# A sliding-window attention with a gated feed-forward on one core: the branch to a general path turned round and hinted, the test's product later, the first tile's row sums elsewhere

## The chip, the cores and the metric

The kernel runs on one core of one Trainium2 chip. The core has a matrix engine (TensorE; PE in the profile, and PEld for its weight loads), three engines for elementwise work (VectorE, DVE; ScalarE, ACT; GpSimd, POOL) and an engine that mainly issues DMAs (SyncE, SP). Each runs its own list of instructions in order and waits for the others by semaphores. The metric is the device time of one execution in microseconds, as the median of several runs.

## The reference

Attention over 8 batches of 8 heads, 576 positions, 64 dimensions, where a position sees itself and the 63 before it; then a gated feed-forward over the 4608 tokens.

```
scores = scale * q @ k^T                 # scale = 1/8
scores = where(0 <= row - column < 64, scores, -1e9)
attn = exp(scores - max);  attn = attn / (sum + 1e-9)
x = (attn @ v), heads side by side       # 4608 x 512
g = x @ w_gate                           # 512 x 1536
out = (g * sigmoid(g) * (x @ w_val)) @ w_out
```

## The kernel before

**Tiles.** The tokens are worked off as nine tiles (NT = 9) of 512. Tile 0 has code of its own; tiles 1 to 6 and 8 hold 512 positions of one batch each; tile 7 (LAST) collects the last 64 positions of all batches. Of each tile the kernel makes the scores, their exponents without taking off the maximum, the row sums by a product with ones, their inverse as exp(-ln(sum)) on ACT, and the attention's output scaled by it (`xT`). Then come twelve gate steps (`gate_value`, matmuls at L470): each makes 128 of the 1536 columns of the gate and value products with eight matmuls of 512 columns, ACT makes the sigmoid-weighted gate (`sg`, L463) and DVE the product with the value (`hT`, L464). The projection with `w_out` (L479, L491, L532) of a tile lies among the next tile's attention; that of the last tile stands at the end, in four blocks of 128 tokens (`project` for three, `project_last` for the fourth), each with a copy out of the accumulator on DVE and output DMAs on SP's queue.

**Order.** The order of the instructions on each engine is that of the program text (a manual schedule). The accumulators are eight banks; a gate step takes two of the four banks 4 to 7 in turn, so the second step after it takes the same two again.

**The start.** For tile 0 the four head pairs u go one after the other: cast, transpose (L207), copy out (L714, L210), scores (L260), exponent (`weigh_first`, L719), row totals (`sums_first`, L326), logarithm (L347), inverse (`invert`, L350), the product with v (L376, L391), and the scaling (L427). The first gate matmuls (`gate_part`, L446) follow as the four parts of `xT` get done.

**The test.** Since no maximum is taken off, an exponent could run over. ACT can sum a row beside its main result (`accum_out`), which costs it a second instruction, ACTIVATION_READ_ACCUMULATOR. Every exponent and every inverse writes such a sum into a column of `spread` (`extent()` gives the next column). In gate step 4 of the last tile `survey` (L539) compares all columns with a bound, takes the minimum over them (`within`), adds the 128 partitions with one matmul of one column (L545) and casts the result into `count`. At the end of the program every engine loads the count into a register (`values_load`, L943). Where it is under 128 (`tc.If`, L944) the general path runs, a long plain version of the whole computation. For the data here it is 128, and the general path is passed over.

**The branch as it is laid out.** `preferred_fallthrough_block=False` puts the block for "not less" next: on each engine a compare-and-branch that is not taken, a few semaphore settlements (EVENT_SEMAPHORE, L944; SP's wait for its outputs to land among them), then a jump over the general path to the closing code (L972: waits, drains, the last barrier).

Of the kernel before, what the change touches and what calls it, by code (L numbers as in the profile page):

```python
# [8 lines left out]
P = 128  # L9
FP32 = mybir.dt.float32  # L10
BF16 = mybir.dt.bfloat16
AF = mybir.ActivationFunctionType
ALU = mybir.AluOpType
PSUM = bass.MemoryType.PSUM


@with_exitstack
def kernel(
# [10 lines left out]
    nc = tc.nc  # L29
    S, D, H = 576, 64, 8  # L30
    NTOK, DFF, DM = 4608, 1536, 512
    NT = NTOK // 512
# [39 lines left out]
    def extent():  # L72
        columns_used[0] += 1
        return spread[:, columns_used[0] - 1:columns_used[0]]
# [153 lines left out]
    def turn_k(dst, k_s, u):  # L228
        nc.vector.transpose(  # L229
            dst[:, u, :].rearrange("r (g x e) -> r g e x", g=4, e=4),  # L230
            k_s[:, :, u].rearrange("r g (e d) -> r g e d", d=D)[:, :, :, 0:32],
        )
# [106 lines left out]
    def room(n):  # L339
        return fsb.tile([P, 2, 512], FP32, name="r", tag="r", bufs=4)[:, 0:n]  # L340
# [5 lines left out]
    def log(r, d_ps):  # L346
        nc.scalar.activation(r, d_ps, AF.Ln, bias=floor[:])  # L347

    def invert(r):
        nc.scalar.activation(r, r, AF.Exp, scale=-1.0, accum_out=extent())  # L350

    def logs(t, r, d):
        if t == NT - 1:
# [4 lines left out]
    def sums(t, w, tiles):  # L358
        r = room(2)
        totals(t, w, tiles if len(tiles) > 1 else [tiles[0][:, x] for x in range(2)])  # L360
        for x in range(2):
            inverse[t, 2 * w + x] = r[:, x]
        if len(tiles) > 1:
            for x in range(2):
                logs(t, r[:, x:x + 1], tiles[x].rearrange("r (b x) -> r b x", b=1))
        else:
            logs(t, r, tiles[0])
        return lambda: invert(r)

    def part_first(us, x, ms, last=None):  # L370

# [94 lines left out]
    def gate_value(t, m):  # L466
        pair = gate_tiles()
        for ps, w in zip(pair, (wg, wv)):
            for c in range(4):
                nc.tensor.matmul(  # L470
                    ps[:], w[:, c, P * m:P * m + P], xT[t][:, c, :],
                    start=(c == 0), stop=(c == 3),
                )
        gate_end(t, m, pair)
# [48 lines left out]
    def project(t, s, o_ps):  # L523
        project_part(t, (s,), (o_ps,), range(12))
        project_end(t, s, o_ps)

    def project_last(t, s):
        r0 = S * batch(t) + P * s
        os_ = fsb.tile([P, 512], FP32, name="os_", tag="os_", bufs=4)
        for f0, f1, o_ps in ((0, 384, bank[6]), (384, 512, bank[0])):  # L530
            for c in range(12):
                nc.tensor.matmul(  # L532
                    o_ps[:, 0:f1 - f0], hT[t][:, c, P * s:P * s + P], wo[:, c, f0:f1],
                    start=(c == 0), stop=(c == 11),
                )
            nc.vector.tensor_copy(os_[:, f0:f1], o_ps[:, 0:f1 - f0])
            nc.sync.dma_start(out[r0:r0 + P, f0:f1], os_[:, f0:f1])

    def survey():  # L539

        used = spread[:, 0:columns_used[0]]
        fine = fsb.tile([P, 64], FP32, name="fine", tag="fine", bufs=1)[:, 0:columns_used[0]]
        nc.vector.tensor_single_scalar(fine, used, MOST, op=ALU.is_le)
        nc.vector.tensor_reduce(within[:, 0:1], fine, axis=mybir.AxisListType.X, op=ALU.min)
        nc.tensor.matmul(two[0][:, 0, 0:1], ones[:, 0:P], within[:, 0:1])  # L545
        nc.vector.tensor_copy(count[:], two[0][:, 0, 0:1])

# [168 lines left out]

    def weigh_first(u):
        E = eb[u][:, 1:17].rearrange("r (h y) z -> r h (y z)", h=2)
        nc.scalar.activation(E, two[u % 2][:], AF.Exp, scale=0.125, accum_out=extent())  # L719
        weights[0, u] = E  # L720

    def sums_first(u, b):
        totals_first(u, bank[b])
        inverse[0, u] = room(1)[:, 0]
        return lambda: log(inverse[0, u], bank[b]), lambda: invert(inverse[0, u])

    cast_first(on_a, 0, 0)
    cast_first(on_v, 0, 1)
# [83 lines left out]
    for m in range(12):  # L812
        if m < 4:
            if m == 2:
                pairs += [gate_tiles(), gate_tiles()]
                for i, w in enumerate((wg, wv)):
                    for n in (2, 3):
                        for c in range(4):
                            gate_one(0, n, pairs[n][i], w, c)
            gate_end(0, m, pairs[m])  # L820
        else:
            gate_value(0, m)
        if m == 3:
            for x in range(2):
                for c in range(2):
                    nc.vector.tensor_copy(
                        mask[half(x), 0, c],
                        tri[half(x), x ^ c].rearrange("r (y e) -> r e y", e=16),
                    )
            for i in (1, 2, 4):  # L830
                nc.vector.tensor_copy(mask[:, i:2 * i], mask[:, 0:i])
            for E in eb:
                nc.vector.memset(E[:, 0], 0.0)
        if m == 10:
            for u in range(4):
                tp = two[u % 2].bitcast(BF16)[:, u // 2, 0:512]
                for e in range(4):
                    for h in range(2):
                        nc.tensor.transpose(  # L839
                            tp[half(h), P * e:P * e + P], raw_k[:, 2 * u + h, e], identb[:]  # L840
                        )
            for u in range(4):
                tp = two[u % 2].bitcast(BF16)[:, u // 2, 0:512]
                split_k(kT[1][:, u, :], tp, on_a if u % 2 else on_v)
        if m == 8:
            second_halves(1, lo, 1, on_v)
            second_halves(1, lo, 0, on_a)
        if m == 9:
            for u in range(2):
                turn_q(1, u)  # L850
# [34 lines left out]
    for t in range(1, NT):  # L885
        if t > 1:
            set_exp()
            masks = scores(t, 0)
            masks[0]()
            project_quads(t - 1, tiles, range(12), 0)  # L890
            for x in range(2):
                marker(4 + 2 * x, x)
            on_a(fence[:], bank[4][0:D, 0:1])
            on_v(seen[:], bank[6][0:D, 0:1])
            masks[1]()
            if t == 2:
                stage_v(3)
            ready(scores(t, 1))
            for x in range(2):
                marker(4 + 2 * x, x)  # L900
            project_quads(t - 1, tiles, range(7), 1)
            end = sums(t, 0, two[0:1])
            project_quads(t - 1, tiles, range(7, 12), 1)
            for w in range(2):
                mix_half(t, w, two[1 - w])
            project_end(t - 1, 0, tiles[0], on_a)
            ends = end, sums(t, 1, (bank[4], bank[6]))
            for end in ends:
                end()
            project_end(t - 1, 2, tiles[2])  # L910
            project_part(t - 1, (1,), (bank[5],), range(12))
            scale_all(t, (two[1], two[0]))
            project_end(t - 1, 1, bank[5], on_a)
            project_part(t - 1, (3,), (bank[4],), range(12))
        set_silu()
        if t > 1:
            project_end(t - 1, 3, bank[4], on_v)
        on_p(past[:], xT[t][:, 3, 0:1])  # L918
        if t + 1 == LAST:
            load_last_v()  # L920
        elif t + 1 < NT and t > 1:
            cast_v(t + 1)
        if t + 2 < NT:
            load_qk(t + 2)
            if t > 1 and t + 2 != LAST:
                stage_v(t + 2)
        if t == 2:
            k_l = cast.tile([P, 4, 4, 4 * D], BF16, name="k_l", tag="c0")
        if t in (2, 3):
            load_k(k_l, [(b, S - P) for b in range(4, 8)], quarters[2 * t - 4:2 * t - 2])  # L930
        turns = (6, 7, 9, 10) if t == 1 else (1, 4, 7, 10)
        for m in range(12):
            gate_value(t, m)
            if t == NT - 1 and m == 4:
                survey()
            if m in turns and t + 1 < NT:
                turn(t + 1, turns.index(m))
            if (t, m) in late:
                turn_k(kT[2], k_l, late.index((t, m)))
    for s in range(3):  # L940
        project(NT - 1, s, bank[(5, 7, 4)[s]])
    project_last(NT - 1, 3)
    good = nc.values_load(count[0:1, 0:1], min_val=0, max_val=P)  # L943
    with tc.If(good < P, preferred_fallthrough_block=False):  # L944
        for b in range(8):
            x_b = general_attention(b)
            general_ffn(b, x_b)
# [29 lines left out]
```

## Time and profile before

| | us |
|---|---|
| median of 3 runs | 330.51 (330.12 to 330.61) |
| the profiled execution's own time | 330.77 |
| its span | 329.05 |
| PE busy | 315.8 |
| first gate matmul starts | 16.07 |
| last matmul ends | 320.85 |
| last copy ends | 321.16 |

The span runs from the first to the last instruction of the program; the execution's own time holds 1.72 us around it. "Busy" counts matmuls, elementwise work and POOL's DMA writing; branches, register loads and semaphore instructions are not counted, so a stretch in which all engines stand at 0 can still be full of these. In the trace such instructions stand under the engine's name with a q (SPq, PEldq). The granted clock of TensorE is 0.993 over the span.

### The profile page before, as it was taken

To read this page: it belongs to the slowest core of one execution; us is meant where nothing else is said; L and a number is where in the kernel's file an instruction comes from. 1 tells how busy PE (TensorE), PEld (TensorE's weight loads), DVE (VectorE), ACT (ScalarE), POOL (GpSimd) and SP (SyncE) were. 2 spreads that over 40 slices of the span, in tenths; PEclk is the share of its full clock that TensorE was granted. 3 is DMA by queue.
4 is the path that set the end of the run, shared out by engine and by line. 5 is a ranking of instruction groups with operands and counts; after the bars stand their busy time and mean duration, and the time that the engine had idled before them with its cause. 6 is when DMAs were issued, how large, how long until landed. Compare 5 with 4: busy or idle time off the path is not lost.

```text
span 329.0 us, 8172 instructions
## 1 busy us (share of the span) xinstructions
PE 315.8 (96%) x3298; PEld 158.9 (48%) x3298; DVE 209.7 (64%) x345; ACT 177.1 (54%) x295; POOL 147.7 (45%) x268
## 2 busy tenths in 40 slices
PE   7899999999999999999999999999999999998990
PEld 3544444446444644464446444644455445543450
DVE  4855846596667657674778477858875587643330
ACT  4964765358534863486338733873377336932200
POOL 3965656867667156624560399027870200000000
PEclk9999999999999999999999999999999999999997
DMA  7999999999699349944991489249995200120031
GB/s 221 213 195 198 208 140 228 200 199 125 124 205 186 52 100 190 193 56 121 170 180 19 120 108 110 29 106 171 178 145 104 54 0 2 47 85 2 1 100 40
DMA packets 83537, 40.53 MB, mean 123 GB/s; under 512 B 64161, under 2 KB 78753, under 8 KB 83489
## 3 DMA queue, kind: packets, MB, share of 16 engines
q0 software_dynamic: 51488, 22.59, 57.4%
q1 hardware_dynamic: 31456, 16.79, 22.6%
q8 instruction: 28, 0.46, 0.6%
q10 hardware_dynamic: 544, 0.52, 0.5%
q14 instruction: 21, 0.16, 0.2%
HBM read 53.02 MB, written 9.44 MB: 190 GB/s over the span
## 4 chain that ended last, share of the span: by engine, by line
PE 94%; DMA 1%; ACT 1%; DVE 1%; issue 0%; DVEq 0%
PE one L470 55%; PE one L479 17%; PE one L491 11%; PE two L289 3%; PE two L411 2%; PE one L446 2%; DMA q_f<-in_q_dram 1%; ACT eb L719 1%; PE two L333 1%; PE one L532 1%; PE two L446 1%; PE one L333 1%; ACT qk_b L705 0%; PE two L839 0%; PE one L207 0%
## 5 line engine op out<-in xcount | busy, mean ns | idle before, releaser
L463 ACT ACTIVATE sg<-one 128x512 f32<-128x512 f32 x107 | 63.9, 597 | 115.7 <-PE one L470 90.2
L464 DVE TENSOR_TENSOR hT<-sg,one 128x512 bf16<-128x512 f32 x107 | 74.0, 693 | 62.9 <-PE one L470 59.3
L470 PE MATMUL one<-xT,wg 128*128 128x512 bf16 x416 | 106.8, 379 | 0.0
L470 PE MATMUL one<-xT,wv 128*128 128x512 bf16 x416 | 106.8, 379 | 0.0
L138 POOL DMA_DIRECT2D k_s<-in_k_dram x112 | 60.5, 563 | 26.6 <-DMA q_s<-in_q_dram 14.9
L470 PEld LDWEIGHTS <-wg 128*128 128x128 bf16 x416 | 40.6, 98 | 50.1 <-issue 1.5
L470 PEld LDWEIGHTS <-wv 128*128 128x128 bf16 x416 | 40.7, 98 | 49.0
L479 PE MATMUL one<-wo,hT 128*128 128x512 bf16 x252 | 56.5, 379 | 0.0
L918 POOL COPY past<-xT 128x1 bf16<-128x1 bf16 x8 | 1.5, 189 | 88.9 <-DVE xT L427 88.9
L491 PE MATMUL one<-wo,hT 64*64 64x512 bf16 x672 | 40.4, 376 | 0.0
L479 PEld LDWEIGHTS <-hT 128*128 128x128 bf16 x252 | 23.8, 98 | 29.3 <-issue 2.0
L229 DVE STREAM_TRANSPOSE kT<-k_s 128x512 bf16<-128x512 bf16 x28 | 36.0, 1287 | 0.0
L427 DVE TENSOR_TENSOR xT<-two,r 128x512 bf16<-128x512 f32 x34 | 21.2, 683 | 22.4 <-ACT r L350 22.4
L304 ACT ACTIVATE eb<-two 128x960 bf16<-128x960 f32 (+1 forms) x32 | 31.0, 973 | 3.8 <-PE two L289 3.7
L491 PEld LDWEIGHTS <-hT 64*64 64x64 bf16 x672 | 21.7, 107 | 10.8
L310 DVE TENSOR_TENSOR eb<-eb,mask 128x960 bf16<-128x960 bf16 (+1 forms) x32 | 21.0, 655 | 8.0 <-ACT eb L304 8.0
L219 DVE STREAM_TRANSPOSE qT<-q_s 128x512 bf16<-128x512 bf16 x32 | 22.3, 700 | 0.1
L350 ACT ACTIVATE r<-r 128x1024 f32<-128x1024 f32 (+1 forms) x20 | 19.3, 970 | 0.1
L315 DVE TENSOR_TENSOR both<-eb 128x512 bf16<-128x512 bf16 x32 | 13.6, 426 | 1.1
L103 POOL DMA_DIRECT2D q_s<-in_q_dram x24 | 13.0, 555 | 2.0 <-DMA v<-in_v_dram 1.1
L164 POOL DMA_DIRECT2D vb<-in_v_dram x16 | 11.0, 693 | 6.1 <-DMA wo<-in_moe_w_out_dram 3.7
L347 ACT ACTIVATE r<-one,floor 128x512 f32<-128x512 f32 x17 | 10.9, 683 | 4.0 <-PE one L333 4.0
(146 smaller groups left out, 259.1 us busy)
## 6 DMA issues: line engine op xcount, KB each, us to landing
k_s<-in_k_dram POOLq DMA_DIRECT2D x112, 56.0 KB, 5.3
q_s<-in_q_dram POOLq DMA_DIRECT2D x24, 248.0 KB, 5.9
v_f<-in_v_dram SPq DMA_DIRECT2D x40, 128.0 KB
wg<-in_moe_w_gate_dram POOLq DMA_DIRECT2D x5, 256.0 KB, 8.1
wv<-in_moe_w_val_dram POOLq DMA_DIRECT2D x5, 256.0 KB, 8.7
q_f<-in_q_dram SPq DMA_DIRECT2D x4, 256.0 KB
wo<-in_moe_w_out_dram POOLq DMA_DIRECT2D x2, 512.0 KB, 10.8
vb<-in_v_dram POOLq DMA_DIRECT2D x16, 64.0 KB, 6.4
```

What stands on the lines that cost most here:

```text
L138: nc.gpsimd.dma_start(k_s[p0:p0 + 32, g, :, 0:w], k[b, a:H:2, s:s + P].rearrange("u (r e) d -> r u (e d)", e=4) [:, :, 32 * c:32 * c + w],)
L219: nc.vector.transpose(queries[t][:, u, :].rearrange("r (e x) -> r e x", e=16), staged[t][0][:, u].rearrange("r (e d) -> r e d", d=D)[:, :, ...
L229: nc.vector.transpose(dst[:, u, :].rearrange("r (g x e) -> r g e x", g=4, e=4), k_s[:, :, u].rearrange("r g (e d) -> r g e d", d=D)[:, :, ...
L304: nc.scalar.activation(flat, s_ps[:].rearrange("r a b -> r (a b)")[:, 0:n], AF.Exp, scale=0.125, accum_out=extent(),)
L310: nc.vector.tensor_mul(flat, flat, mask[:].rearrange("r j c e y -> r (j c e y)")[:, 0:n])
L350: nc.scalar.activation(r, r, AF.Exp, scale=-1.0, accum_out=extent())
L427: nc.vector.tensor_mul(x, o_ps, r)
L463: nc.scalar.activation(sg[:], g_ps[:], AF.Silu)
L464: nc.vector.tensor_mul(hT[t][:, m, :], sg[:], v_ps[:])
L470: nc.tensor.matmul(ps[:], w[:, c, P * m:P * m + P], xT[t][:, c, :], start=(c == 0), stop=(c == 3),)
L479: nc.tensor.matmul(o_ps[:], hT[t][:, c, P * s:P * s + P], wo[:, c, :], start=(c == 0), stop=(c == 11),)
L491: nc.tensor.matmul(tiles[s][half(y)], hT[t][half(x), c, r0:r0 + 64], wo[half(x), c, :], start=not back and c == 0, stop=bool(back) and c = ...
```

## The change

Three things are changed.

- **The branch.** `preferred_fallthrough_block=True` puts the general path next, and the block that passes it over behind it. The branch is then taken for the data here. It gets a label, and a hint for that label is placed on all five engines after the second of the last tile's four projection blocks: it takes a register value, `P - good`, where 0 tells the engine that the branch will be taken and that the code at its target should be fetched. The load of `good` stands before the last tile's projections instead of behind them, and a check of its bounds is left out.
- **The product.** The matmul over `within` and the cast into `count` become `tally`, called after gate step 7 of the last tile. The comparison and the minimum stay in step 4.
- **The first tile's sums.** `weigh_first` and tile 0's `invert` give no sum any more. In gate steps 1, 5, 6 and 7 of tile 0 `survey_first` takes the maximum of each row of the exponents on DVE (1024 16-bit values), and copies the inverse onto itself on ACT with a sum. The number of columns in `spread` stays the same.

```diff
+EVERY = tuple(
+    getattr(mybir.EngineType, n) for n in ("PE", "SP", "DVE", "Activation", "Pool")
+)
...
-    def invert(r):
-        nc.scalar.activation(r, r, AF.Exp, scale=-1.0, accum_out=extent())
+    def invert(r, **kept):
+        nc.scalar.activation(r, r, AF.Exp, scale=-1.0, **kept)
...
-        return lambda: invert(r)
+        return lambda: invert(r, accum_out=extent())
...
         nc.vector.tensor_reduce(within[:, 0:1], fine, axis=mybir.AxisListType.X, op=ALU.min)
+
+    def tally():
+
         nc.tensor.matmul(two[0][:, 0, 0:1], ones[:, 0:P], within[:, 0:1])
         nc.vector.tensor_copy(count[:], two[0][:, 0, 0:1])
...
-        nc.scalar.activation(E, two[u % 2][:], AF.Exp, scale=0.125, accum_out=extent())
+        nc.scalar.activation(E, two[u % 2][:], AF.Exp, scale=0.125)
         weights[0, u] = E
...
         inverse[0, u] = room(1)[:, 0]
+        firsts[u] = inverse[0, u]
         return lambda: log(inverse[0, u], bank[b]), lambda: invert(inverse[0, u])
+
+    firsts = {}
+
+    def survey_first(u):
+
+        nc.vector.tensor_reduce(
+            extent(), eb[u][:, 1:17].rearrange("r s z -> r (s z)"),
+            axis=mybir.AxisListType.X, op=ALU.max,
+        )
+        nc.scalar.activation(firsts[u], firsts[u], AF.Copy, accum_out=extent())
...
+        if m in (1, 5, 6, 7):
+            survey_first((1, 5, 6, 7).index(m))
...
             if t == NT - 1 and m == 4:
                 survey()
+            if t == NT - 1 and m == 7:
+                tally()
...
+    good = nc.values_load(
+        count[0:1, 0:1], min_val=0, max_val=P,
+        skip_runtime_bounds_check_because="a count of 128 partitions",
+    )
     for s in range(3):
         project(NT - 1, s, bank[(5, 7, 4)[s]])
+        if s == 1:
+            tc.mark_branch_hint_location("settled", P - good, engines=EVERY)
     project_last(NT - 1, 3)
-    good = nc.values_load(count[0:1, 0:1], min_val=0, max_val=P)
-    with tc.If(good < P, preferred_fallthrough_block=False):
+    with tc.If(good < P, preferred_fallthrough_block=True, label="settled"):
```

## The prediction

> **What bounds the kernel now.** I read the page first, then the chain of waits, then the timeline around each hole in it, then two lines of the source (the branch, L944, and the program's closing line, L972), and last the stretches after the last matmul. The page shows where to look:
>
> ```profile
> span 329.0 us, 8172 instructions
> ...
> PE 315.8 (96%) x3298; PEld 158.9 (48%) x3298; DVE 209.7 (64%) x345; ACT 177.1 (54%) x295; POOL 147.7 (45%) x268
> ...
> PE one L470 55%; PE one L479 17%; PE one L491 11%; PE two L289 3%; PE two L411 2%; PE one L446 2%; DMA q_f<-in_q_dram 1%; ACT eb L719 1%; PE two L333 1%; PE one L532 1%; PE two L446 1%; PE one L333 1%; ACT qk_b L705 0%; PE two L839 0%; PE one L207 0%
> ```
>
> TensorE is busy for 96% of the span, and the change takes no matmul away. It can only gain where PE stands: at the start, in a hole, or after the end. From 16.07 us, the first gate matmul, the chain stays with PE except for one place:
>
> ```profile
> 288.34 8.65 PE one L470 x40
> ...
> 297.08 0.69 DVE hT L464
> ...
> 297.90 0.23 DVE within L544
> ...
> 298.17 0.16 PE two L545
> 298.33 12.11 PE one L470 x56
> ```
>
> PE reaches the test's product (L545) at 296.98 and needs `within`, which DVE makes only after the gate product in front of it. Gate steps that lie 1.727 us apart (hT at 293.62, 295.35, 297.08) are 3.11 us apart here (297.08 to 300.19).
>
> The last matmul ends at 320.85 and the last copy at 321.16, yet the span goes to 329.05. This tail of 7.9 us shows in two source lines (count, shortest/median/longest ns, first and last start):
>
> ```profile
> L944 ACTq COMPARE_BRANCH  x2: 38/44/49, 310.1 to 310.3; - x2
> L944 PEldq COMPARE_BRANCH  x2: 95/1939/3783, 319.6 to 321.0; - x2
> ...
> L944 SPq COMPARE_BRANCH  x2: 38/46/53, 322.6 to 324.6; - x2
> ```
>
> ```profile
> L972 SPq EVENT_SEMAPHORE  x14: 17/28/28, 327.4 to 329.0; - x14
> ...
> L972 ACTq DRAIN  x2: 8/44/80, 312.8 to 328.5; - x2
> ```
>
> and in the stretches after it (the last two figures are the DMA engines' busy share and GB/s):
>
> ```profile
> 322.40:323.40 1.00, 0.00 (x0) 0.00 (x0) 0.00 (x0) 0.00 (x0) 0.00 (x0) 1.00 0.13 32
> 323.40:323.90 0.50, 0.00 (x0) 0.00 (x0) 0.00 (x0) 0.00 (x0) 0.00 (x0) 1.00 0.06 7
> ...
> 325.20:326.50 1.30, 0.00 (x0) 0.00 (x0) 0.00 (x0) 0.00 (x0) 0.00 (x0) 0.50 0.09 25
> ```
>
> Each engine has two branch instructions: the test, which falls into a short block of semaphore settlements, and a jump over the general path to the closing code. After the jump every engine is silent for 2.5 to 3.8 us: SP from 324.61 to 327.39 (2.79), ACT from 310.3 to 312.8, DVE from 321.75 to 324.72 (2.97); PE's jump itself is recorded as 3.78. In each gap lies a packet of 8 or 16 KB on an instruction queue. So a far jump costs an instruction fetch, and SP's comes last, because SP settles only after the last output has landed at 324.48. That landing is late too: 15 of its 16 shares were in at 322.86. The sixteenth share's eight 512-byte packets ran from 323.39 to 323.85, right behind PE's own 16 KB fetch (322.44 to 323.41). I read this as PE's fetch holding one DMA engine.
>
> **The change part by part.**
>
> *The product later.* `within` is ready at 298.1 and the product now stands behind gate step 7, about 302; nothing waits. Gain 3.11 - 1.727 = 1.38, less a matmul of one column. The nearest row for what that holds PE are the markers (L398, 0.03 in the chain); with its weights (0.10) I take 0.05. **-1.33**. Cover: DVE has 1.04 us idle per step for the 0.16 us CAST.
>
> *Reading `good` earlier.* The loads (TENSOR_LOAD 0.46 to 0.54, FUSED_REGOPS 0.19 on SP) now stand on every queue before the last projections. PE: its queue was 1.57 us ahead of the array (load at 319.04, last matmul starting at 320.61), and the load plus register work is 0.7. The step before lets it run as far ahead (step 11's value matmuls may issue when hT of step 9 ends, 307.8; the array ends at 310.44), so 0; without that cover it costs at most 0.7. DVE has 1.8 us idle before each of the last copies, ACT and POOL have no work left, and SP waits for copies anyway: 0. Queued behind them are the last output copies and DMAs, which come with 1.3 to 1.9 us to spare. The assertion (0.04) goes. On SP this also takes 0.93 us (321.64 to 322.57) from between the last DMA and the branch.
>
> *The hint.* One register subtraction and one instruction on each queue between the third-last and second-last output block. No row shows a hint. The nearest are FUSED_REGOPS 0.19 and COMPARE_BRANCH 0.04 to 0.10, hence 0.2 to 0.3, under the same covers: 0. A gain of its own is excluded at that place; what it may do to the supply of code is a rival below.
>
> *The branch.* The general path now follows, and the settlements and closing code lie behind it. SP would branch right after its last DMA issue (ends 321.59) at 321.65.
> With the target already fetched: eight settlements at 0.07 to 0.08 each end at 322.3; SP waits for the last landing. PE's fetch is no longer at 322.4, so I take the fifteen shares' 322.86 to SP's other landings' 2.1 after issue (323.3). The closing code then runs without a second far jump: 322.95 to 323.4 in place of 327.39, and from there to the end stay the 1.66 us of before. Gain 4.0 to 4.4; I take **-4.2**. Next late then is the output DMA itself.
> Without a working hint: SP's jump misses at 321.65 and returns at 324.5 (2.8); eight settlements take 0.56; the closing code starts at 325.06. Gain 2.33. The miss now lies beside the landing instead of behind it.
>
> *The first tile's row sums.* Eight ACTIVATION_READ_ACCUMULATORs leave the start (L719 x4, L350 x4). Each is recorded with 0.2 but costs ACT 0.1: the exponent of 7.74 has its read at 8.65, and the next instruction starts at 8.75. ACT is almost without a gap from 7.0 to 17.6, so the bounds are 0 and 0.8. Step by step: the first read gives 0.08, but the second totals then stand behind PE's bias matmuls (10.37 plus two of 0.22, and their latency) and come at 10.95 for 11.09; the second logarithm is at 11.40 for 11.54; without two reads behind it the third exponent starts at 12.65 for 12.88 and its result is out at 13.70 for 14.03. There PE waited (0.42 idle on `eb`), and from there it runs through to the first gate matmul: **-0.33**. The weights allow it: the tightest, `wv` for steps 2 and 3, land at 19.80 and are needed at 20.9; the key rows of the second tile land at 34.45 for 34.8.
>
> What comes in its place: four DVE reductions of 1024 elements and four ACT copies with sums, in steps 1, 5, 6, 7. No row has such a reduction. L544 (56 elements) takes 0.215, L427 0.68 for 512 elements, which makes about 1.04 ns an element; estimate 0.15 + 1.07 = 1.22. (The fast end would be L310's 0.66 for 960, the slow end L791's 0.66 for 512, 1.31.) DVE's idle time is 1.34 in step 1 and 1.04 in steps 5 to 7, so hT slips by 0.2 a step, 0.6 in all (0.8 at the slow end), and steps 8 and 10 have 0.59 and 0.83 to give it back. PE needs hT of a step only 1.8 us after it is made, when the bank is taken again: 0. Without that cover, 0.6. ACT: a copy is 0.6 and the read 0.1 against 1.13 idle; in step 1 only 0.26 is idle and one sigmoid slips by 0.44, with 2 us free behind it: 0.
>
> The Trainium skill ("VectorE: DVE Perf Modes", the table of operations) says that a reduction has no faster mode for 16-bit data; by that rule the fast end is out and the term stays 0, since the estimate is already at one element a cycle.
>
> **Sum.** 1.33 + 0.33 + 4.2 = 5.86. The profiled execution took 330.77 (span 329.05 plus 1.72 around it): 324.91. The median, 330.51, is 0.26 lower: **324.65**. 0.2%, about what a measurement of this kernel can tell from no change, is 0.7 us.
>
> **The rivals.**
> 1. *The hint doesn't help SP.* Either it is not followed, or the closing code (some 30 instructions from the target) crosses into a block that is fetched only on arrival. For it: no run here shows a hint at work, and every far jump recorded misses. Against: SP has 4.6 us between the hint and the branch, and a fetch with its restart took 2.8. Not followed: 330.51 - 1.33 - 0.33 - 2.33 = 326.5. Crossing: closing code at about 324.5, gain 2.9, 325.95.
>  The Trainium skill ("Runtime: NRT & Kernel Launch", instruction fetch mechanics) calls the prefetch purely sequential, with a taken branch outside a window of two pages forcing a fetch. The jump gaps above agree with the second half; by the first half this rival's 326.5 would come out.
> 2. *The hinted block displaces the next one in sequence on PE.* PE crosses into a new block late (a 16 KB instruction packet at 318.0). It would then stall among the last matmuls: 3.78 less the 1.57 it is ahead, +2.2, and the jump would miss as well: 326.5 + 2.2 = 328.7.
> 3. *Slower: the same displacement, repeated.* If fetching back the next block also drops the one behind it, PE pays 3.78 twice and only one run-ahead covers it: +6.0, 326.5 + 6.0 = 332.5. It decides against the change from +4.0, which a second miss reaches. Against it: in 300 us of straight code no row shows PE waiting for code for more than 0.43 us (an "issue" gap at 247.6).
> 4. *No change.* Only a partial displacement that eats just the 4.0 of rival 1's gains.
>
> **How the numbers follow.** Hint works: 0.60, 324.65, with 324.2 to 325.2 as its own range (start gain 0 to 0.5, tail 4.0 to 4.4). Rival 1: 0.27, 325.9 to 326.9 (with no gain at the start). Rival 2: 0.06. Rival 3: 0.05. Rival 4: 0.02. The range 324.2 to 327.0 takes in the forecast and rival 1, 0.87 less their tails. Faster 0.93, same 0.02, slower 0.05.
>
> **What would show it.** hT steps of 1.73 throughout the last tile. First gate matmul near 15.7. SP's closing code (L972) within 0.3 of the last landing; the branch records on all engines short, PE's 3.78 gone; no 16 KB instruction packet between the last output DMA's issue and its landing. A gap of 2.8 between SP's test and its first settlement means rival 1; a PE hole with an instruction packet after the hint means 2 or 3. The prediction is wrong by most if the tail holds another wait than the fetch, for instance if the landing at 324.48 is late without PE's fetch (then only 2.8 of the tail goes).

## The result, and the profile after

The changed kernel takes 325.96 us in the median (325.73 to 326.30); the kernel before, timed beside it, 330.31. The ratio is 0.987, with a 95% interval of 0.9853 to 0.9887: faster by 1.3%. The profiled execution took 325.93 us with a span of 324.2, so it stands at its own median, while that of before (330.77) stood 0.26 above the median it was read against.

The page of the changed kernel, its first lines and its chain by line:

```profile
span 324.2 us, 8153 instructions
...
PE 314.4 (97%) x3267; PEld 158.4 (49%) x3298; DVE 213.7 (66%) x349; ACT 178.8 (55%) x295; POOL 147.7 (46%) x268
...
PE one L473 45%; PE one L482 14%; PE one L494 11%; DMA wv<-in_moe_w_val_dram 3%; DMA wo<-in_moe_w_out_dram 3%; PE two L292 3%; DMA q_s<-in_q_dram 2%; PE two L414 2%; DMA wg<-in_moe_w_gate_dram 2%; DMA vb<-in_v_dram 2%; POOL k_s L141 1%; DMA q_f<-in_q_dram 1%; PE one L535 1%; POOL v L159 1%; PE one L336 1%
```

The page has 1.4 us less of TensorE than before, but also 31 fewer records of its matmuls (x3267 for x3298), and the change takes no matmul away: some are missing from this trace, and its chain runs over DMAs instead, probably for that reason. The second profile of the same kernel (last of the experiments) has all 3298, with 316.5 us for 315.8 before and 95% of the chain on PE. So TensorE is as busy as before, the span is 4.8 us shorter, and what went was standing time. Four stretches add up to the two spans: from the start to ACT's first cast (which waits for the first rows of q), from there to the first gate matmul, from there to the end of the last matmul, and the tail from there to the end of the span.

| us | before | after | difference |
|---|---|---|---|
| start to the first cast | 5.17 | 4.53 | -0.64 |
| cast to the first gate matmul | 10.90 | 10.68 | -0.22 |
| gate matmul to the end of the last matmul | 304.76 | 303.17 | -1.59 |
| tail | 8.22 | 5.83 | -2.39 |
| span | 329.05 | 324.21 | -4.84 |

The first row is the landing of a DMA that the change doesn't touch; in the other kernels below it lies between 4.46 and 4.92.

**The hole in the last tile** is gone. The chain of waits of the changed kernel from 288 us on (start, length, what):

```profile
293.12 7.93 PE one L473 x36
301.05 0.00 PE two L551
301.06 2.83 PE one L473 x13
...
317.70 0.68 PE two L535 x12
318.39 0.02 issue
318.41 0.29 DVE os__4697 L539
```

The test's product (L551) stands at 301.05 among the gate matmuls and waits for nothing. The greatest distance between two hT products of the last tile is 1.75 us, for 3.11 before.

**The tail.** The branch is L970 now; its lines in the view by source line (count, shortest/median/longest ns, first and last start):

```profile
L970 SPq EVENT_SEMAPHORE  x8: 17/17/17, 322.0 to 322.5; - x8
...
L970 PEldq COMPARE_BRANCH  x1: 1577/1577/1577, 316.6 to 316.6; - x1
...
L970 DVEq COMPARE_BRANCH  x1: 84/84/84, 318.4 to 318.4; - x1
L970 SPq COMPARE_BRANCH  x1: 70/70/70, 319.2 to 319.2; - x1
L970 DVEq EVENT_SEMAPHORE  x1: 21/21/21, 321.8 to 321.8; - x1
```

and the closing code and the hints, L998:

```profile
L998 SPq EVENT_SEMAPHORE  x14: 17/28/28, 322.6 to 324.1; - x14
...
L998 PEldq BRANCH_PREFETCH_HINT  x1: 49/49/49, 309.3 to 309.3; - x1
L998 DVEq BRANCH_PREFETCH_HINT  x1: 55/55/55, 313.4 to 313.4; - x1
L998 SPq BRANCH_PREFETCH_HINT  x1: 54/54/54, 314.5 to 314.5; - x1
```

SP branches at 319.19, and its first settlement comes at 321.98: a gap of 2.80, the price of a far jump, though the hint had been given 4.7 us ahead. DVE shows the same, 3.4 us after a hint 5.0 us ahead. TensorE's record shrank from 3.78 to 1.58. By the time SP has settled, at 322.54, the last output has landed (321.96), so the closing code starts at once, at 322.58. SP jumps beside the landing and not behind it, and sooner, since the count is loaded already; that is all the branch gave.

In the stretches after the last matmul the engines stand at 0 and only DMA engines work (the last two columns are their busy share and GB/s; the third last is the granted clock):

```profile
319.20:320.40 1.20, 0.00 (x0) 0.00 (x0) 0.00 (x0) 0.00 (x0) 0.00 (x0) 1.00 0.65 210
320.40:321.50 1.10, 0.00 (x0) 0.00 (x0) 0.00 (x0) 0.00 (x0) 0.00 (x0) 1.00 0.08 15
321.50:322.60 1.10, 0.00 (x0) 0.00 (x0) 0.00 (x0) 0.00 (x0) 0.00 (x0) 1.00 0.03 7
```

From 320.40 to 321.50 the last shares of the outputs are still on their way, alone, as in the kernel before. The DMA view for the 0.4 us from the start of the last output's issue shows what was in its way, an instruction packet of 16 KB on TensorE's queue:

```profile
q8 instruction: 1, 0.02, 24.3%
q1 hardware_dynamic: 6, 0.01, 6.3%
```

It runs from 318.83 to 320.38, and the late share's packets start at 320.37. I read this as one DMA engine that works off first the one and then the other; the packet records here don't name their engine, the times are the evidence.

**The start.** The reductions and the copies that came into tile 0:

```profile
L738 DVE TENSOR_REDUCE spread<-eb 128x1 f32<-128x1024 bf16 x4 | 4.9, 1213 | 0.0
```

```profile
L742 ACT ACTIVATE r<-r 128x512 f32<-128x512 f32 x4 | 2.5, 621 | 0.0
L742 ACT ACTIVATION_READ_ACCUMULATOR r<-r 128x1 f32 x4 | 0.8, 192 | 0.0
```

A reduction takes 1.21 us. Against before, hT comes 0.86 us earlier in the first step of tile 0 and 0.80 earlier in step 4: beside the gate steps they cost nothing that lasts. The Trainium skill ("VectorE: DVE Perf Modes", the table of operations) gives a reduction no fast mode; 1.21 us for 1024 16-bit values agrees.

### The profile page after: what moved, and what is told of

The parts are those of the page before. It is cut to its first block, busy times and chain, and to the rows that moved or that the text cites. A ratio compares the mean times of both kernels' runs of the same rounds, so it can differ in the third digit from the quotient of the medians.

```text
span 324.2 us, 8153 instructions
## 1 busy us (share of the span) xinstructions
PE 314.4 (97%) x3267; PEld 158.4 (49%) x3298; DVE 213.7 (66%) x349; ACT 178.8 (55%) x295; POOL 147.7 (46%) x268
## 4 chain that ended last, share of the span: by engine, by line
PE 77%; DMA 14%; POOL 4%; issue 2%; DVE 1%; SPq 0%; POOLq 0%
PE one L473 45%; PE one L482 14%; PE one L494 11%; DMA wv<-in_moe_w_val_dram 3%; DMA wo<-in_moe_w_out_dram 3%; PE two L292 3%; DMA q_s<-in_q_dram 2%; PE two L414 2%; DMA wg<-in_moe_w_gate_dram 2%; DMA vb<-in_v_dram 2%; POOL k_s L141 1%; DMA q_f<-in_q_dram 1%; PE one L535 1%; POOL v L159 1%; PE one L336 1%
## 5 line engine op out<-in xcount | busy, mean ns | idle before, releaser
L473 PE MATMUL one<-xT,wg 128*128 128x512 bf16 x405 | 104.7, 379 | 0.1
L482 PE MATMUL one<-wo,hT 128*128 128x512 bf16 x241 | 55.4, 379 | 0.7 <-issue 0.3
```

Source lines behind the costliest of these rows:

```text
L473: nc.tensor.matmul(ps[:], w[:, c, P * m:P * m + P], xT[t][:, c, :], start=(c == 0), stop=(c == 3),)
L482: nc.tensor.matmul(o_ps[:], hT[t][:, c, P * s:P * s + P], wo[:, c, :], start=(c == 0), stop=(c == 11),)
```

## The experiments

The theory formed from these two traces: the three parts add up as separate stretches, and the hint does nothing for SP. What it would take for a hint to act was the open question, with three rivals: a longer lead in time; an entry into a new block of code between hint and branch, since code comes in packets of 8 KB (SP, DVE, ACT, POOL, on one queue) and 16 KB (TensorE); or a greater number of instructions between them.

### The parts one by one

**The first tile's row sums as before**, all else changed:

```diff
-        nc.scalar.activation(E, two[u % 2][:], AF.Exp, scale=0.125)
+        nc.scalar.activation(E, two[u % 2][:], AF.Exp, scale=0.125, accum_out=extent())
...
-        return lambda: log(inverse[0, u], bank[b]), lambda: invert(inverse[0, u])
+        return lambda: log(inverse[0, u], bank[b]), lambda: invert(inverse[0, u], accum_out=extent())
...
-        if m in (1, 5, 6, 7):
-            survey_first((1, 5, 6, 7).index(m))
```

> The changed kernel with the first tile's row sums where they were (accum_out on its exponents and inverses, no reductions and copies in the gate steps). From the prediction: the first gate matmul comes 0.33 us later counted from ACT's first cast (10.68 us in the changed kernel's profile, 10.90 before), so 10.9 to 11.1, and the time is 0.2 to 0.4 above the changed kernel: 326.2 to 326.4. Rival 'the start's whole 0.86 us between the two profiles is the row sums': 326.8.

Measured: 326.52 us (326.15 to 328.60), 0.9917 (0.9885 to 0.9949). The first cast and the first gate matmul in the timeline:

```profile
4.56 0.62 ACT L711 CAST qk_b<-q_f 128x512 bf16<-128x512 f32 x1 [1.40 <-DMA q_f<-in_q_dram]
```

```profile
15.46 0.39 PE L449 MATMUL one<-xT,wg 128*128 128x512 bf16 x1
```

10.90 us lie between them, exactly as in the kernel before. Without the sums it is 10.53 or 10.54 in those four kernels below whose full granted clock begins as early as in these two (why this counts, the next kernel shows). So the sums cost **0.37 us** at the start. The changed kernel's own profile, with a later clock, has 10.68. The medians, 326.52 for 325.96, are no better measure: the runs scatter by 2.4 us, for a reason that the next kernel shows.

**The product as before**, behind gate step 4:

```diff
-            if t == NT - 1 and m == 7:
                 tally()
```

> The changed kernel with the product back in gate step 4. By the prediction 1.3 to 1.4 us above the changed kernel, 327.3, with the gate steps around it 3.11 us apart instead of 1.73. Rival 'the hole is filled by work that is late elsewhere': under 0.7 us.

Measured: 328.49 us (327.44 to 328.98), 0.9938 (0.9913 to 0.9962). The chain has its hole again:

```profile
297.54 0.69 DVE hT L467
...
298.36 0.23 DVE within L547
...
298.63 0.16 PE two L551
```

hT steps are 3.11 us apart there for 1.73: **1.38 us**. That leaves 1.2 of the 2.5 in the medians; the two fastest runs (327.44, 327.58) stand 1.5 and 1.6 above the changed kernel's median. Its profile has the rest at the start: 12.08 us from cast to gate matmul. One of the warming products there, in this kernel and in the changed one:

```profile
6.56 0.64 PE L674 MATMUL one<-ones 128*64 128x512 bf16 x1
```

```profile
5.90 0.40 PE L674 MATMUL one<-ones 128*64 128x512 bf16 x1
```

0.64 us for 0.40: TensorE worked slower in the first 9.5 us, before any part of the edit was reached. In the traces the records of a full granted clock begin between 3.7 us (before) and 9.7 us (this kernel) after the start of the span, differently in each run, and the interval from cast to gate matmul goes with it. In the kernels with these warming products and without the sums it is 10.53 or 10.54 where the full clock begins at 5.4 us or sooner (four kernels), then 10.68 at 5.6, 10.77 at 5.9, 11.01 and 11.15 at 6.5 and 12.08 at 9.7. The kernel before (3.7) and the one with its sums put back (4.5) belong beside the first four. So the product is read from its place, and 1.5 us of scatter must be allowed to any median here.

**The branch as before**, with the product and the sums changed:

```diff
-    good = nc.values_load(
-        count[0:1, 0:1], min_val=0, max_val=P,
-        skip_runtime_bounds_check_because="a count of 128 partitions",
-    )
...
-        if s == 1:
-            tc.mark_branch_hint_location("settled", P - good, engines=EVERY)
...
-    with tc.If(good < P, preferred_fallthrough_block=True, label="settled"):
+    good = nc.values_load(count[0:1, 0:1], min_val=0, max_val=P)
+    with tc.If(good < P, preferred_fallthrough_block=False):
```

> The changed kernel with the branch of before: settlements next, a jump over the general path at the end, the count loaded at the end, no hint. By the tails of the two profiles (8.20 us from the last matmul's end before, 5.82 after) 2.4 us above the changed kernel: 328.4. If the layout were worth the prediction's 4.2 us: 330.2.

Measured: 328.37 us (327.94 to 329.03), 0.9947 (0.9928 to 0.9966): 2.41 above the changed kernel, and its tail is 8.06 for 5.83. Its source lines:

```profile
L965 PEldq COMPARE_BRANCH  x2: 95/1934/3772, 317.5 to 318.9; - x2
...
L965 SPq COMPARE_BRANCH  x2: 38/46/53, 320.5 to 322.4; - x2
```

```profile
L993 SPq EVENT_SEMAPHORE  x14: 17/28/28, 325.1 to 326.7; - x14
```

SP's jump at 322.44 follows the landing again, and the closing code 2.7 later. The load of the count stands behind the last issue again too: from 319.54 to 320.47 SP loads, works on the register and checks the bounds, 0.93 us that the changed kernel doesn't spend there. As SP's way sets the end of the changed kernel, I estimate from these rows that some 0.9 of the 2.4 belong to the earlier load and the rest to the order of the blocks; no run has the one without the other.

**No hint at all**, the branch turned round:

```diff
-        if s == 1:
-            tc.mark_branch_hint_location("settled", P - good, engines=EVERY)
```

> The changed kernel without its hint, on all five engines. My theory: a hint only decides what the next prefetch brings, and a prefetch happens when an engine enters a new block of code. TensorE enters one between its hint and its branch, SP and DVE do not, so only TensorE's hint did anything. Then SP's gap from branch to first settlement stays 2.8 us; TensorE's branch, recorded with 1.58 us, goes back to 3 us or more, but TensorE is back by 320.5, before SP's 322.0; time 325.8 to 326.1, no difference to the changed kernel. Rival 'no hint does anything': the same time, and TensorE's branch stays 1.6. Rival 'hints help everywhere a little': the time rises by more than 0.5 us.

Measured: 326.23 us (325.88 to 326.46), 0.9867 (0.9843 to 0.9891), the changed kernel's time. SP's gap is 2.72 for 2.80. The hint did act on TensorE, whose record is long again without it:

```profile
L968 PEldq COMPARE_BRANCH  x1: 3932/3932/3932, 316.8 to 316.8; - x1
...
L968 SPq COMPARE_BRANCH  x1: 45/45/45, 319.8 to 319.8; - x1
L968 PEldq EVENT_SEMAPHORE  x1: 51/51/51, 320.8 to 320.8; - x1
```

But TensorE is through at 320.8, before the last landing, so nobody waits for it. All that the branch gave came from the order of the blocks and the earlier load; the hint as placed gave nothing that can be measured in the time.

### What a hint needs

**The hint on SP and DVE 16.5 and 9.5 us ahead of the branch**, right behind the load of the count; TensorE's stays, ACT and POOL have none:

```diff
+    tc.mark_branch_hint_location("settled", P - good, engines=EVERY[1:3])
     for s in range(3):
...
-            tc.mark_branch_hint_location("settled", P - good, engines=EVERY)
+            tc.mark_branch_hint_location("settled", P - good, engines=EVERY[:1])
```

> SP's and DVE's hint right behind the load of the count: SP's 17 us ahead of its branch (4.7 in the changed kernel) but in the same, last block of code; TensorE's as in the changed kernel. My theory (block entry decides): SP's gap stays 2.8 us, 326.0. Rival 'the hint came too late': the gap goes and the time falls to 325.3 as in the early run.

Measured: 326.27 us (325.87 to 326.50), 0.987 (0.9845 to 0.9896), no gain:

```profile
L971 SPq EVENT_SEMAPHORE  x8: 17/17/17, 322.3 to 322.8; - x8
...
L971 SPq COMPARE_BRANCH  x1: 70/70/70, 319.5 to 319.5; - x1
L971 DVEq EVENT_SEMAPHORE  x1: 21/21/21, 322.1 to 322.1; - x1
```

SP's hint stands at 302.93 and its branch still pays 2.80. Nearly 12 us more of lead changed nothing. In SP's order it now stands 12 instructions ahead of the branch (7 in the changed kernel), on DVE 14 (8).

**The hint on SP and DVE at the start of tile 6**, by a register that holds a constant 0, so that the engines are told "taken" long before the count is known (`none` is set to 0 in gate step 9 of tile 0):

```diff
+        if t == 6:
+            zero = nc.values_load(
+                none[0:1, 0:1], engines=EVERY[1:3], min_val=0, max_val=P,
+                skip_runtime_bounds_check_because="a constant",
+            )
+            tc.mark_branch_hint_location("settled", zero, engines=EVERY[1:3])
...
-            tc.mark_branch_hint_location("settled", P - good, engines=EVERY)
+            tc.mark_branch_hint_location("settled", P - good, engines=EVERY[:1])
```

> SP's and DVE's hint placed at the start of tile 6 (with a register that holds zero), before each of them enters its last block of code; TensorE's hint as in the changed kernel; ACT and POOL have none. My theory: SP's gap of 2.8 us between branch and first settlement goes (0.2 or less), DVE's 3.4 too; SP then waits for the last landing, which comes at about 321.8 since TensorE's fetch behind its target still holds one DMA engine; closing code 0.6 to 0.8 us earlier: about 325.3. Rival 'SP's hint is without effect wherever it stands': 326.0 and the gap stays.

Measured: 325.18 us (324.79 to 325.35), 0.9836 (0.9812 to 0.9861).

```profile
L979 SPq EVENT_SEMAPHORE  x8: 17/17/17, 319.7 to 321.8; - x8
...
L979 DVEq COMPARE_BRANCH  x1: 90/90/90, 318.4 to 318.4; - x1
L979 DVEq EVENT_SEMAPHORE  x1: 21/21/21, 319.1 to 319.1; - x1
L979 SPq COMPARE_BRANCH  x1: 70/70/70, 319.2 to 319.2; - x1
```

Here the hint acts: SP's gap is 0.53 for 2.80, DVE's 0.62 for 3.4. SP then waits at its settlements for the landings, until 321.78, and the closing code follows at 321.84. The landing sets the end now.

**The same, and no hint on TensorE:**

```diff
-        if s == 1:
-            tc.mark_branch_hint_location("settled", P - good, engines=EVERY[:1])
```

> As the run before, but TensorE has no hint, so that its two fetches move behind its branch. My theory: they fall at about 318.0 and 321, beside the last output's transfer at 320.0 to 320.5, so the last landing comes at 320.6 to 321.0 instead of 321.8, and with SP's jump hit the closing code starts at about 321.0: 1.5 us under the changed kernel, 324.4. If TensorE's fetch is not what holds the last landing: as the run before, 325.3.

Measured: 324.96 us (324.70 to 325.73), 0.9836 (0.9808 to 0.9864). Expected was a TensorE packet out of the landing's way and 0.9 us less than with the early hint alone; it is 0.2 less, within the scatter. The branch takes 4.27; the packet behind it ran from 318.28 to 319.21, earlier, and instead of the last output's share it held a share of the one before and SP's last DMA issue, which took 1.06 us for the usual 0.38.

**The early hint, and 30 more instructions on TensorE at the start**, to move its entries into blocks of code against the hint:

```diff
-    for _ in range(9):
+    for _ in range(24):
         nc.tensor.matmul(
-            warm[0:D], nc.const_aps.tensor(1.0, [P, D], BF16),
-            nc.const_aps.tensor(1.0, [P, 512], BF16),
+            warm[0:D, 0:192], nc.const_aps.tensor(1.0, [P, D], BF16),
+            nc.const_aps.tensor(1.0, [P, 192], BF16),
```

> The early run (SP's and DVE's hint at tile 6, TensorE's after the second projection block) with 30 more instructions on TensorE at the very start: the nine warming products of 512 columns are 24 of 192, the same columns. TensorE's blocks of code then shift by 30 instructions, so that it enters its last one soon after its hint, near 310 instead of 315. My theory: its target is there when it branches at 316.6 (record 0.1 instead of 1.6), the fetch behind the target falls at 317.3 to 318.3, before the last two outputs are in flight, and these land 2.1 us after issue, at 320.9 instead of 321.8. Closing code at 321.0, time 0.8 under the early run: 324.4. If TensorE's fetch doesn't hold the landing: 325.2 as the early run.

Measured: 325.47 us (324.71 to 327.13), 0.9874 (0.9837 to 0.9911), the expected 324.4 missed. The entry moved as meant: the 16 KB packet follows the hint by 2.5 us for 6.4, and the branch, which comes well after it, takes 0.41 for 1.58. The next packet (318.66 to 319.54) then met SP's last issue: the two issues of L541 take 1.32 us together,

```profile
318.60 1.32 SPq L541 DMA_DIRECT2D out_dram<-os__4700  x2
```

for this in the kernel with the early hint alone:

```profile
318.35 0.81 SPq L541 DMA_DIRECT2D out_dram<-os__4685  x2
```

But no share is late in it, and the tail is 4.62 us, 0.46 less than with the early hint alone. The profiled execution took 324.99, with 10.83 from cast to gate matmul; the median is drawn up by runs of 325.96 and 327.13, which left no trace.

**The same with 70 more instructions**: 44 warming products of 104 columns for nine of 512, by the same two lines.

> The nine warming products of 512 columns are replaced by 44 of 104 columns, which puts 70 more instructions into TensorE's sequence ahead of everything else: TensorE should enter its last block of code some 26 instructions before its hint instead of some 40 behind it. Theory (a hint only redirects the prefetch made on entering a block): TensorE's 16 KB packet comes at about 307 to 309, before the hint, brings the next block in sequence, and TensorE's branch is recorded with 3.3 to 4.3 us, as where it has no hint (3.93 and 4.27), although the hint stands 7 us ahead of it; that miss lies after the last projections' products have been issued and its 16 KB fetch at about 318.3 to 319.3 may hold the last output's issue or a share as in the run without TensorE's hint: 325.0 to 325.7. Rival (TensorE's hint acts by its lead of 7 us, SP's and VectorE's fail for another reason): the branch stays at 0.4 to 1.6 us.

Measured: 326.47 us (326.21 to 326.70), 0.9875 (0.9844 to 0.9905). Both were missed: the branch takes 0.50, not 3.3 to 4.3, and the time is 0.8 over the range. That lies elsewhere: 11.45 us from cast to gate matmul, with a wait of 0.72 for `v` to land among them, and a stand of TensorE that no wait explains, 1.05 us where the other runs have 0.60 at most (start, length):

```profile
248.63 1.05 issue
```

Two 16 KB packets come here, 0.35 and 4.7 us behind the hint, where the other kernels have one. The first lies too close to the hint to tell which it is.

**170 more instructions** settle it for TensorE: 94 products of 48 columns.

> 94 warming products of 48 columns in place of nine of 512: 170 more instructions ahead of everything else on TensorE, so that it enters its last block of code some 126 instructions (about 10 us) before its hint and meets no further block until its branch. Theory (a hint only redirects the prefetch made on entering a block, on every engine; in the run with 44 products the entry lay too close to the hint to tell): one 16 KB packet at about 295 to 303, none between the hint at about 311 and the branch at about 318, and the branch is recorded with 3.3 to 4.3 us. Rival (TensorE's hint brings its target whenever it comes): a 16 KB packet 0.3 to 5 us behind the hint, and the branch takes 0.4 to 0.6.

One execution: 328.73 us, of which 11.82 from cast to gate matmul; from 16.0 to 19.3 us TensorE's granted clock is 0.50 in this trace alone, so the time says nothing about the hint. The branch does. The DMA view for the 8.7 us up to the hint at 313.27 holds no packet of TensorE's (q8); its last one came at 303.3. From the hint to the branch it holds one, at 314.3:

```profile
q8 instruction: 1, 0.02, 0.9%
q14 instruction: 1, 0.01, 0.3%
```

```profile
L979 PEldq COMPARE_BRANCH  x1: 403/403/403, 320.5 to 320.5; - x1
```

The rival's case, to the letter: a packet 1.0 us behind the hint, and a branch of 0.40. TensorE needs no entry into a block to follow a hint. So my theory of block entries, which had fitted the runs before these two, falls as a rule for every engine.

**The early hint and the changed kernel once more, side by side.**

> The kernel with the early hint on SP and VectorE once more, beside the changed kernel itself on the same chip. Theory: SP's jump returns after 0.5 us and lies beside the landing; 325.2 by the first runs, 0.6 to 0.8 below the changed kernel. Rival (the first runs differed by their starts alone): the same time as the changed kernel within 0.2.

> The changed kernel, unchanged, as the yardstick for the early hint: 325.9 to 326.0, with SP's first settlement 2.7 us after its branch.

Measured: 325.84 us (325.12 to 327.36), 0.986 (0.9831 to 0.9889), for the early hint, and 326.33 (325.81 to 328.16), 0.9886 (0.9855 to 0.9917), for the changed kernel. The medians differ by 0.49 and the fastest runs by 0.69, less than the scatter of either. The profiles leave no doubt on the place, though: SP's gap is 0.53 for 2.91, and the tail 5.23 for 5.95 (the first time 5.07 for 5.83).

What a hint needs, then:

| engine, kernel | hint ahead of the branch | branch is which instruction after the hint | gap or record (us) |
|---|---|---|---|
| SP, as changed | 4.7 us | 7 | 2.80 |
| SP, behind the load | 16.5 us | 12 | 2.80 |
| SP, tile 6 | 130.8 us | 82 | 0.53 |
| DVE, as changed | 5.0 us | 8 | 3.41 |
| DVE, behind the load | 9.5 us | 14 | 3.4 |
| DVE, tile 6 | 111.6 us | 182 | 0.62 |
| ACT and POOL, as changed | 0.1 us | 1 | 2.6, 2.7 |
| PE, as changed, and with 30, 70, 170 more ahead | 7.2 us | 73 | 1.58, 0.41, 0.50, 0.40 |
| PE, without | | | 3.93, 4.27 |

Shown: a lead of 16.5 us is not enough on SP, and 7.2 are on TensorE, so no one lead in time holds for both. Every hint that acted has its branch 73 or more instructions behind it, every one that failed 14 or fewer. **What stays open** is whether the number of instructions decides, or a rule of its own on each engine, be it a longer lead (on SP something between 16.5 and 130.8 us) or an entry into a block: no run has a hint on SP at 20 to 70 instructions, or one on TensorE close to its branch, and since SP, DVE, ACT and POOL fetch on one queue, the traces don't tell whose packet is whose there. The early hint also reads another register than the late ones; both hold 0, and TensorE's hint acts with the late one's. Open is also what sets the time from TensorE's hint to its packet, 6.4 us as changed, 2.5 with 30 instructions more and 1.0 with 170.

The Trainium skill ("Runtime: NRT & Kernel Launch", instruction fetch mechanics) calls the prefetch purely sequential, and says that a taken branch out of a window of two pages forces a fetch. For SP and DVE as changed that held. It did not for TensorE in any run with a hint, nor for SP and DVE with the early one; there the measurement decides.

## Why the prediction was right or wrong

It gave 324.65 with a range of 324.2 to 327.0, and 325.96 came out: the sign and the range held, the point was 1.3 too low. The range held because it took in the first rival, that the hint doesn't help SP, and this rival is what came. That the time stands beside the 325.95 of this rival's milder case, in which only the closing code is fetched late, is luck: the traces show its other case, the hint not followed at all, which it put at 326.5. Of the 0.5 between, 0.2 is the kernel before, which ran faster here than the median that this was taken from, 0.1 is what the three parts brought beyond this case's sum, and the rest is the size of what the start does from run to run.

- *The product later*, -1.33: 1.36. The hole put back is 1.38, and the extra matmul, taken at 0.05, shows as one hT step of 1.75 among those of 1.73. Right.
- *The first tile's row sums*, -0.33: 0.37. Right, by the steps given. What came in their place cost nothing, as said; a reduction takes 1.21 us for the 1.22 estimated. The first gate matmul came at 15.21 for "near 15.7", since the first landing was 0.64 sooner.
- *Reading `good` earlier*, 0: TensorE's load (at 305.39) is followed by no hole. Right. The 0.93 that it takes out of SP's way was counted in the branch, and there it is some 0.9 of the gain.
- *The branch*, -4.2: **this is the term that failed.** It gave 2.39 in the profiles and 2.41 by the branch put back, against 2.33 worked out for a hint that doesn't help. Two of its steps were wrong. The first is "with the target already fetched", held up against the rival by SP's 4.6 us between the hint and the branch, where a fetch takes 2.8. The hint did nothing for SP, not even 16.5 us ahead, and the sign named to tell the rival, a gap of 2.8 between SP's branch and its first settlement, was there: 2.80. Where SP's hint acts, the tail is 5.07 for 5.83 and 5.23 for 5.95. So this step is 0.7 to 0.8 of the 1.8 that the term was over.
- *The landing* is the second step, and the larger, some 1.1. TensorE's packet was expected out of its way, and the last landing 2.0 to 2.5 us after the last matmul (322.86 to 323.3, with the matmul's end at 320.83). The packet comes 0.45 us behind the last matmul now (1.6 before), between the last issue and the landing, and holds a share as before: the last output lands 3.20 us after its issue, for 3.28, and 3.6 after the last matmul (3.4 with the early hint). Even with SP's hint at work the tail is 5.1 to 5.2, and with TensorE's packet moved as well 4.5 to 4.6, never the 4.0 that 8.2 less 4.2 would have been. "SP's closing code within 0.3 of the last landing" failed too (0.63); with the early hint it is 0.08.
- *The other rivals.* TensorE never stands for more than 0.05 us between a hint and its last matmul, in any run, with a packet or without: no displaced code.

The sum closes: 1.36 + 0.37 + 2.39 is 4.12 of the 4.35 between the medians. The rest, 0.2, is the size of what the start does from run to run; in the two profiles, 4.84 apart, the rest is mostly the 0.64 of the first landing.

The kernels that do best have SP's and DVE's hint in tile 6: 325.18 and 325.84 in two sets of runs, and 324.96 with none on TensorE beside it, for the changed kernel's 325.96 and 326.33. Among the kernels with the early hint the differences lie within the scatter.

## What to carry to other kernels

A far branch at the kernel's end cost its engine 2.4 to 4.3 us here; lay the blocks so that the jump that is always taken comes ahead of the last wait, not behind it, and load what it tests early. A prefetch hint is only there if the gap behind the branch says so (0.5 against 2.8 us on SP here), and moving it earlier in time within the same dozen instructions changed nothing. Read a change of a microsecond at its own place in the trace when the start of the kernel scatters by more than that.

## What the runs showed of the hardware that I had not expected

- **An instruction packet holds up a share of an output, as one DMA engine would that takes them in turn.** The late share of an output starts within 0.02 us of the end of TensorE's 16 KB packet in seven kernels: packet end 323.41 and late packets from 323.39 before, 320.38 and 320.37 after; then 319.35 and 319.34 (no hint), 320.18 and 320.17 (early hint), 319.21 and 319.19 (early, none on TensorE), 320.53 and 320.52 (behind the load), 321.28 and 321.26 (branch put back).
- **It can hold up the issue of a DMA too.** The second of SP's last two issues, begun inside such a packet, ends 0.37 to 0.38 us behind the packet's end: it takes 0.72 us (no hint), 1.06 (early, none on TensorE), 0.89, 1.00 and 1.01 (30, 70 and 170 instructions more), for 0.38 outside. Not every issue inside a packet is held: the one of the changed kernel at 316.51, 2.6 us behind the issue before it, lies inside the packet of 315.76 to 316.64 and takes 0.36. With the last issue held, the same packet costs either a share (tail 5.07) or an issue (tail 4.62).
- **TensorE's speed at the start differs from run to run**: 0.40 or 0.64 us for the same product, and up to 1.5 us from cast to first gate matmul, in kernels that are alike up to there. It goes with the time at which the full granted clock is first recorded, 4.1 to 9.7 us into the span in these.
